# Fourier mixing before a mixture of experts: transforms without twiddle factors, and their 64x64 products in quarters of TensorE

## The chip, the cores and the metric

One core of a Trainium2 chip. Inputs and outputs lie in the chip's memory (HBM). The metric is the device time of one execution in microseconds. The kernel before takes 1613.09 us (median of 3 runs, 1611.04 to 1615.54).

## What is computed

```
batch, seq, dim = 8, 2496, 256;  N, D, E, F = 19968, 256, 8, 1024
X = np.fft.rfft(x, axis=1)                       # along the sequence
y = np.fft.irfft(X * (filt_r + 1j * filt_i), n=2496, axis=1)
x = y.reshape(N, D)
logits = x @ w_gate;  expert_idx = argmax(logits);  gate_w = softmax(logits)[expert_idx]
h = np.maximum(x_e @ w1[e], 0.0)                 # the rows of each expert e
out = gate_w[:, None] * (h @ w2[e])              # in the order of the tokens
```

All data is fp32. The kernel has two halves: a filter over the sequence, by a transform, a product and the transform back, for each of eight batches; and one expert of eight for each of the 19968 rows.

## The kernel before

*Filter.* 2496 is 39 x 64. A transform over 2496 points is made of 64 transforms over 39 points (stage A) and then, for each f of 0 to 19, one over 64 points (stage B); the remaining 19 values of f follow by symmetry, since x is real. Real and imaginary parts are rows of their own. The 256 columns of the data are the moving operand throughout, and the tables of cosines and sines are the weights.

- `stage_a` (L338): the three positions of the 64 that fill 117 rows at a time are multiplied by `tas` (117 x 120), 512 columns at a time (L344). The result `zo` goes to HBM (`zd`), because the next stage needs another distribution over partitions.
- `stage_b` (L351): for two values of f, two products of 256 columns with the 128 x 128 table of that f (L359). The twiddle factors, which a split into 39 and 64 needs, are in this table, so that there is one per f (`tbs`, 20 tables). Then VectorE multiplies by the filter: the product with its real part (L366), two products of half the partitions with its imaginary part, crosswise (L367, L368), and the sum (L370; in batch 0 on GpSimd).
- `stage_c` (L373): the 64-point transform back, with one table for all f but 0 (L384; L382 for f = 0 and 1), stored as `ud`.
- `stage_d` (L393): the 39-point transform back with a table for each of 22 groups (`tds`, which holds twiddle factors too), two products of 256 columns into a bank (L405), copied out as `yo`.
- `turn_y`, `logits`, `turn_logits`, `route` (L471 to L622): the result is turned and multiplied by `w_gate` (L491, four products of 32 output columns, in four strips of TensorE's columns), the expert and the row's place are found, and GpSimd scatters the rows to HBM, sorted by expert (L607).

Batch 0 goes another way, without HBM between the stages: `first_a` (L424), `turn_z` (L441), `stage_b`, `first_c` (L449), `turn_u` (L464) with the data kept in SBUF as `zt` and `ut`, turned by TensorE.

*Experts.* Tiles of 512, 256 and at the end 128 rows of one expert: `rows_in` loads them, `turn_x` (L737) turns them, `hidden` (L744) and `result` (L758) multiply with `w1` and `w2`, L748 and L763 evacuate, and GpSimd scatters to the output (L764).

*Order.* The order of TensorE, VectorE, ScalarE and the queue of SP is written out by the program (L913); GpSimd's is set by a scheduler. `slot(k)` lists the steps of the filter in which batch k is in stages B and C, batch k + 1 in A and batch k - 1 in D and the routing; each step has a place between 0 and 1 and a cost in us. A clock `now` advances by these costs. Between steps of the filter, expert steps are taken in: each filter step earns `share()` (L907, between 0.3 and 4) times its cost as credit. `stage_c` for one pair of f stands behind `stage_b` for the next. `either` (L234) gives each evacuation to VectorE or ScalarE, whichever would be free first by the program's reckoning; `stage_b` adds its vector work to that reckoning (L371). PSUM banks come from a pool of seven (L188), loads of x, z and u from a pool of seven buffers (`NIN`, L302).

Of the kernel before, what the change touches and what calls it, by code (L numbers as in the profile page):

```python
# [19 lines left out]
P = 128  # L20
S = 2496
# [3 lines left out]

N1 = 39
N2 = 64
NF = (N1 + 1) // 2
NS = 2 * NF

NB = 3
NG = 22
# [3 lines left out]
FT = F // P  # L36


def dft_tables():

    w = 2.0 * np.pi
    q = np.arange(N1)
    t = np.arange(N2)
    g = np.arange(N2)  # L50
    half = N2 // 2
    sg = np.where(g < half, 1.0, -1.0)

    ta = np.zeros((NB, N1, NB, NS))
    for f in range(NF):
        ang = w * ((q * f) % N1) / N1
        for j in range(NB):
            ta[j, :, j, f] = np.cos(ang)
            if f:
                ta[j, :, j, NF + f] = -np.sin(ang)  # L60

    tb = np.zeros((2, N2, NF, 2, N2))
    for f in range(NF):
        ang = w * ((t[:, None] * (f + N1 * g)[None, :]) % S) / S
        c, sn = np.cos(ang), np.sin(ang)
        if f:
            tb[0, :, f, 0] = c
            tb[1, :, f, 0] = sn
            tb[0, :, f, 1] = -sn * sg
            tb[1, :, f, 1] = c * sg  # L70
        else:
            tb[0, :, f, 0, :half] = c[:, :half]
            tb[0, :, f, 1, 1:half] = -sn[:, 1:half]
            tb[0, :, f, 0, half] = (-1.0) ** t

    tc = np.zeros((2, N2, 2, 2, N2))
    ang = w * ((g[:, None] * t[None, :]) % N2) / N2
    c, sn = np.cos(ang), np.sin(ang)
    tc[0, :, 1, 0] = c
    tc[0, :, 1, 1] = sn  # L80
    tc[1, :, 1, 0] = -sn * sg[:, None]
    tc[1, :, 1, 1] = c * sg[:, None]
    tc[0, :half, 0, 0] = 2.0 * c[:half]
    tc[1, :half, 0, 0] = -2.0 * sn[:half]
    tc[1, 0, 0, 0] = 0.0
    tc[0, 0, 0, 0] = 1.0
    tc[0, half, 0, 0] = (-1.0) ** t

    td = np.zeros((NB, NS, NG, NB, N1))
    ids = np.zeros((NB, N1, NG))  # L90
    valid = np.zeros((NB, N1, NG))
    for j in range(NB):
        for i in range(len(range(j, N2, NB))):
            n = N2 * q + NB * i + j
            ids[j, :, i] = n
            valid[j, :, i] = 1.0
            td[j, 0, i, j] = 1.0 / S
            for f in range(1, NF):
                ang = w * ((n * f) % S) / S
                td[j, f, i, j] = 2.0 / S * np.cos(ang)  # L100
                td[j, NF + f, i, j] = -2.0 / S * np.sin(ang)

    return {
        "ta": ta.reshape(TP, TK),
        "tb": tb.reshape(P, NF, P),
        "tc": tc.reshape(P, 2, P),
        "td": td.reshape(TK, NG, TP),
        "ids": ids.reshape(TP, NG),
        "valid": valid.reshape(TP, NG),
    }  # L110


def lay_x(x):

    out = np.zeros((x.shape[0], P, NG, D), x.dtype)
    v = x.reshape(-1, N1, N2, D)
    for j in range(NB):
        n = len(range(j, N2, NB))
        out[:, j * N1:(j + 1) * N1, :n] = v[:, :, j::NB]
    return out  # L120


def lay_filter(fr, fi):

    g = np.arange(N2)[:, None]
    f = np.arange(NF)[None, :]
    k = f + N1 * g
    k = np.where(k <= S // 2, k, S - k)
    fr, fi = fr[k], fi[k]
    h = NF // 2  # L130
    return np.concatenate([np.concatenate([fr, fr]), np.concatenate([fi[:, :h], fi[:, h:]])], axis=1)
# [3 lines left out]
def kernel(  # L135
# [3 lines left out]
    filt: bass.AP,  # L139
# [5 lines left out]
    tcm: bass.AP,  # L145
    td: bass.AP,
    ids: bass.AP,
# [48 lines left out]
    tbs = cst.tile([P, NF, P], F32, name="tbs")  # L196
    tcs = cst.tile([P, 2, P], F32, name="tcs")
    tds = cst.tile([TK, NG, TP], F32, name="tds")

    ht = cst.tile([P, NF + NF // 2, D], F32, name="ht")  # L200
# [14 lines left out]
    pro = first.enter_context(tc.tile_pool(name="pro", bufs=2, side="right"))  # L215
    pools = {}
# [33 lines left out]
    FH = [(f0, 4) for f0 in range(0, NF, 4)]  # L250


    def load_filters(c):
        f0, n = FH[c]
        nc.sync.dma_start(out=tbs[:, f0:f0 + n], in_=tb[:, f0:f0 + n])
        nc.sync.dma_start(out=ht[:HP, f0:f0 + n], in_=filt[:HP, f0:f0 + n, :])
        half, f1 = divmod(f0, NF // 2)
        rows = slice(half * HP, (half + 1) * HP)
        nh = min(n, NF // 2 - f1)
        nc.sync.dma_start(out=ht[rows, NF + f1:NF + f1 + nh], in_=filt[rows, NF + f1:NF + f1 + nh, :])  # L260
        if nh < n:
            nc.sync.dma_start(out=ht[HP:, NF:NF + n - nh], in_=filt[HP:, NF:NF + n - nh, :])
        if c == 0:
            nc.sync.dma_start(out=tcs, in_=tcm)

    def load_rest():
        nc.sync.dma_start(out=tds, in_=td)
        nc.vector.memset(wg, 0.0)
        nc.sync.dma_start(out=wg[:, :, :E], in_=moe_w_gate.rearrange("(i p) e -> p i e", p=P))
        nc.sync.dma_start(out=ids0, in_=ids)  # L270
        nc.sync.dma_start(out=vld, in_=valid)
# [21 lines left out]
    def columns(ap, i0, n):  # L293

        rows = ap.rearrange("t s d -> (t s) d")
        m = min(n, NG - 1 - i0)
        yield TK, slice(0, m), rows[i0 * TK:(i0 + m) * TK, :].rearrange("(i p) d -> p i d", p=TK)
        if m < n:
            yield NS, slice(m, n), rows[(NG - 1) * TK:, :].rearrange("(i p) d -> p i d", p=NS)
# [26 lines left out]
    def load_z(b, c):  # L326
        f0, n = FH[c]
        zi = fin(("z", b, c))
        nc.sync.dma_start(out=zi[:HP, :n], in_=zd[b][:, f0:f0 + n, :])
        nc.sync.dma_start(out=zi[HP:, :n], in_=zd[b][:, NF + f0:NF + f0 + n, :])  # L330

    def load_u(b, c):
        i0, n = CH[c]
        ui = fin(("u", b, c))
        for r, m, v in columns(ud[b], i0, n):
            nc.sync.dma_start(out=ui[:r, m], in_=v)

    def stage_a(b, c):  # L338
        i0, n = CH[c]
        xt = ins.pop(("x", b, c))  # L340
        zo = sb.tile([TK, 4, D], F32, tag="st", name="zo", bufs=4)
        for j in range(0, n, 2):
            p = bank()
            mm(p[:TK, :], lhsT=tas, rhs=xt[:TP, j:j + 2, :], start=True, stop=True)  # L344
            evac(zo[:, j:j + 2, :], p[:TK, :].rearrange("p (t d) -> p t d", t=2), 512)
        for r, m, v in columns(zd[b], i0, n):
            move(v, zo[:r, m])
# [3 lines left out]
    def stage_b(b, f):  # L351
        c, j = divmod(f, 4)
        if b == 0:
            zi, j = outs.pop(("zi", f)), 0
        else:
            zi = ins["z", b, c] if j == 0 else ins.pop(("z", b, c))
        p = bank()
        for i in range(2):
            mm(p[:, i * D:(i + 1) * D], lhsT=tbs[:, f + i, :], rhs=zi[:, j + i, :], start=True, stop=True)  # L359

        z2 = p.rearrange("p (i d) -> p i d", i=2)
        ys = outs["y", b, f] = sb.tile([P, 2, D], F32, tag="ys", name="ys", bufs=3)
# [618 lines left out]
```

## Time and profile before

| | |
|---|---|
| median of 3 runs | 1613.09 us |
| profiled execution, its own time | 1628.11 us |
| span in the profile | 1626.4 us |
| mean granted TensorE clock | 0.987 |
| TensorE busy | 1570.7 us, 7094 instructions |
| weight loads busy | 1143.6 us |
| VectorE, ScalarE, GpSimd busy | 423.1, 518.5, 358.2 us |
| expert products L744, L758 | 592.0 + 503.9 + 83.2 us busy |
| filter products L344, L359, L384, L405 | 74.5, 73.2, 67.0, 77.6 us busy |
| moved by DMA | 289.89 MB, mean 178 GB/s |

A group in the profile is a line, an engine, an operation and the tiles: `bank<-ys,tcs` is a product with moving operand ys and table tcs into a PSUM bank. "Busy" counts overlapping instructions once; a "mean ns of one" contains the instruction's latency, so that a pipelined instruction appears longer than its share of the time. Text in brackets or after the second bar says how long the engine was idle before, and whose end released it. A fp32 product appears as two matmul instructions, a transposition as one. In the timeline, slot 0 begins at 18.7 us (the first L441), slot 1 about 56 us, slot 2 about 125 us, slot 3 about 195 us, slot 4 about 300 us; the first expert tile is turned at 164.5 us, and after some 1050 us only experts are left.

### The profile page before, as it was taken

To read this page: it belongs to the slowest core of one execution; us is meant where nothing else is said; L and a number is where in the kernel's file an instruction comes from. 1 tells how busy PE (TensorE), PEld (TensorE's weight loads), DVE (VectorE), ACT (ScalarE), POOL (GpSimd) and SP (SyncE) were. 2 spreads that over 40 slices of the span, in tenths; PEclk is the share of its full clock that TensorE was granted. 3 is DMA by queue.
4 is the path that set the end of the run, shared out by engine and by line. 5 is a ranking of instruction groups with operands and counts; after the bars stand their busy time and mean duration, and the time that the engine had idled before them with its cause. 6 is when DMAs were issued, how large, how long until landed. Compare 5 with 4: busy or idle time off the path is not lost.

```text
span 1626.4 us, 21714 instructions
## 1 busy us (share of the span) xinstructions
PE 1570.7 (97%) x7094; PEld 1143.6 (70%) x7094; DVE 423.1 (26%) x1418; ACT 518.5 (32%) x1149; POOL 358.2 (22%) x373
## 2 busy tenths in 40 slices
PE   8988899999999999999999899999999999999998
PEld 6645667787566666666666566667666678889997
DVE  4676571624412422235222111300000000000000
ACT  4434343333322232322233232122222222333433
POOL 1131312404213321023213205411111011111111
PEclk9999999999999999999999999999999999999999
DMA  9679796887935584357434624433344347565551
GB/s 283 185 198 293 234 329 196 244 262 241 289 121 163 167 250 138 114 152 191 144 106 129 178 89 142 145 112 112 133 151 153 129 142 229 187 214 184 172 182 46
DMA packets 119700, 289.89 MB, mean 178 GB/s; under 512 B 17387, under 2 KB 58484, under 8 KB 119469
## 3 DMA queue, kind: packets, MB, share of 16 engines
q1 hardware_dynamic: 100373, 245.18, 49.9%
q0 software_dynamic: 19216, 43.33, 7.7%
q8 instruction: 58, 0.95, 0.2%
q14 instruction: 53, 0.43, 0.1%
HBM read 208.44 MB, written 80.90 MB: 178 GB/s over the span
## 4 chain that ended last, share of the span: by engine, by line
PE 90%; DMA 4%; DVE 3%; issue 2%; SPq 0%; ACT 0%; POOL 0%; POOLq 0%; ACTq 0%; DVEq 0%
PE bank L758 34%; PE bank L744 34%; PE bank L405 4%; PE bank L359 3%; PE bank L344 3%; PE bank L384 3%; PE bank L737 2%; PE bank L477 2%; DMA fin<-zd 1%; PE lt L491 1%; DMA fin<-ud 1%; DMA ud<-uo 1%; PE bank L424 1%; DVE yw L368 1%; DVE yw L367 1%
## 5 line engine op out<-in xcount | busy, mean ns | idle before, releaser
L744 PE MATMUL bank<-xT,w1t 128*128 128x512 f32 (+2 forms) x2080 | 592.0, 436 | 0.0
L758 PE MATMUL bank<-w2t,hT 128*128 128x256 f32 x2240 | 503.9, 382 | 2.6 <-issue 2.6
L744 PEld LDWEIGHTS bank<-xT,w1t 128*128 128x128 f32 x2080 | 338.9, 191 | 206.2 <-issue 183.7
L758 PEld LDWEIGHTS bank<-w2t,hT 128*128 128x128 f32 x2240 | 423.9, 191 | 70.2 <-issue 14.2
L764 POOL DMA_INDIRECT out_dram<-ys,idt x163 | 160.6, 985 | 917.2 <-ACT ys L763 624.4
L748 ACT ACTIVATE hT<-bank 128x512 f32<-128x512 f32 (+2 forms) x520 | 227.3, 438 | 369.3 <-PE bank L744 333.4
L607 POOL DMA_INDIRECT rows<-yo,row x176 | 175.5, 997 | 303.5 <-DVE row L587 73.6
L763 ACT ACTIVATE ys<-bank,gts 128x256 f32<-128x256 f32 x157 | 74.3, 474 | 500.0 <-PE bank L758 447.9
L241 DVE COPY xT<-bank 128x128 f32<-128x128 f32 (+2 forms) x53 | 25.1, 473 | 586.1 <-PE bank L737 459.6
L366 DVE TENSOR_TENSOR ys<-bank,ht 128x512 f32<-128x512 f32 x80 | 55.1, 689 | 131.0 <-PE bank L359 88.2
L405 PE MATMUL bank<-fin,tds 120*117 120x256 f32 (+1 forms) x308 | 77.6, 391 | 12.0 <-DMA fin<-ud 12.0
L758 PE MATMUL bank<-w2s,hT 128*128 x368 | 83.2, 379 | 0.0
L405 PEld LDWEIGHTS bank<-fin,tds 120*117 120x117 f32 (+1 forms) x308 | 55.6, 185 | 37.0 <-issue 20.4
L384 PE MATMUL bank<-ys,tcs 128*128 128x512 f32 x126 | 67.0, 614 | 10.8 <-DVE ys L370 6.1
L344 PE MATMUL bank<-fin,tas 117*120 117x512 f32 x154 | 74.5, 603 | 0.0
L758 PEld LDWEIGHTS bank<-w2s,hT 128*128 128x128 f32 x368 | 68.1, 190 | 8.3
L359 PE MATMUL bank<-fin,tbs 128*128 128x256 f32 x280 | 73.2, 385 | 0.8 <-DMA fin<-zd 0.8
L359 PEld LDWEIGHTS bank<-fin,tbs 128*128 128x128 f32 x280 | 52.3, 192 | 21.5 <-issue 15.5
L241 ACT COPY uo<-bank 128x512 f32<-128x512 f32 x70 | 41.1, 587 | 62.7 <-PE bank L384 36.7
L367 DVE SCALAR_TENSOR_TENSOR yw<-bank,ht 64x512 f32<-64x512 f32 x80 | 55.4, 693 | 1.1
L368 DVE TENSOR_TENSOR yw<-bank,ht 64x512 f32<-64x512 f32 x80 | 54.7, 684 | 1.1
L241 ACT COPY yo<-bank 117x512 f32<-117x512 f32 x70 | 40.6, 589 | 40.7 <-PE bank L405 38.5
(126 smaller groups left out, 877.6 us busy)
## 6 DMA issues: line engine op xcount, KB each, us to landing
w1t<-in_moe_w_dram SPq DMA_DIRECT2D x130, 512.0 KB
w2t<-in_moe_w_dram SPq DMA_DIRECT2D x84, 512.0 KB
fin<-in_x_dram SPq DMA_DIRECT2D x40, 512.0 KB
fin<-zd SPq DMA_DIRECT2D x70, 256.0 KB
ud<-uo SPq DMA_DIRECT2D x70, 256.0 KB
zd<-zo SPq DMA_DIRECT2D x35, 480.0 KB
fin<-ud SPq DMA_DIRECT2D x35, 480.0 KB
xg<-rows SPq DMA_DIRECT2D x28, 544.0 KB
```

Source lines behind the costliest of these rows:

```text
L241: either(n, lambda: nc.vector.tensor_copy(o, i), lambda: nc.scalar.copy(out=o, in_=i))
L344: mm(p[:TK, :], lhsT=tas, rhs=xt[:TP, j:j + 2, :], start=True, stop=True)
L359: mm(p[:, i * D:(i + 1) * D], lhsT=tbs[:, f + i, :], rhs=zi[:, j + i, :], start=True, stop=True)
L367: nc.vector.scalar_tensor_tensor(out=yw[:HP], in0=z2[HP:], scalar=-1.0, in1=fi, op0=ALU.mult, op1=ALU.mult)
L384: mm(p, lhsT=tcs[:, 1, :], rhs=ys, start=True, stop=True)
L405: mm(p[:TP, i * D:(i + 1) * D], lhsT=tds[:k, i0 + j + i, :], rhs=ui[:k, j + i, :], start=True, stop=True)
L607: sc = nc.gpsimd.indirect_dma_start(out=rowsd, out_offset=bass.IndirectOffsetOnAxis(ap=at, axis=0), in_=what, in_offset=None,)
L744: mm(p[:, :m], lhsT=w1t[2 * i + k // FH2][:, dh, k % FH2 * P:(k % FH2 + 1) * P], rhs=xts[i][:, dh, :m], start=(dh == 0), stop=(dh == DH - 1))
L748: lambda: nc.scalar.activation(hT[:, :m], p[:, :m], AF.Relu))
L758: mm(p[:, :D], lhsT=hs[i][k][:, j * P:(j + 1) * P], rhs=w2, start=(k == 0), stop=(k == FT - 1))
L763: lambda: nc.scalar.activation(ys, p[:, :D], AF.Copy, scale=gate))
L764: nc.gpsimd.indirect_dma_start(out=out, out_offset=bass.IndirectOffsetOnAxis(ap=idt[i].bitcast(U32)[:, j, :], axis=0), in_=ys, in_offset=None,
```

## The change

Since 39 and 64 have no common factor, the 2496 positions can be indexed by their remainders, and then the two-dimensional transform needs no twiddle factors. One table serves all f in stage B, one all groups in stage D.

- Positions t and t + 32 of the 64 are added and subtracted first (`add_x`, on GpSimd; the difference of batch 0 on VectorE); the sums give the even, the differences the odd half of the 64-point transform, each over 32 points. Real and imaginary parts of 32 points are 64 rows, so a table is 64 x 64.
- `stage_a` keeps its 512 moving columns a product; its two products of a chunk are the sums and the differences.
- `stage_b` now handles four values of f (q = 0 to 4) at a time: four products of 64 x 64 with 512 columns, in the four quarters of TensorE: o (even or odd half) chooses the rows and the PSUM bank, e (which two of the four f) the output partitions. The filter: a multiplication by the real part for each bank on VectorE (128 x 512), eight copies of 32 x 512 on ScalarE that exchange real and imaginary part, one multiplication by the imaginary part with its sign (128 x 1024) on VectorE, the sum (128 x 1024) on GpSimd.
- `stage_c` is four quarter products likewise, and two evacuations. In batch 0, `first_c` uses a table of 128 x 128 with zeros (`tc0`).
- `stage_d` multiplies one 512-column operand of both halves with the one table; ScalarE copies the even half out, VectorE adds and subtracts the odd half.
- The filter comes in two tables, `hr` and `hi` (128 x 20 x 256 each); GpSimd multiplies `hi` by signs as it is loaded. The copies of the filter on ScalarE in batch 0 (L435) are gone.
- z is loaded and u stored in four DMAs for each q (before: two for each four f). `share()` may reach 12. Small tiles of `tile_map` are shared, and `ys` of the experts has three buffers for four.

```
     def load_filters(q):
...
+        nc.sync.dma_start(out=hr[:, q], in_=filt_r[:, q])
+        nc.sync.dma_start(out=hi[:, q], in_=filt_i[:, q])
+        nc.gpsimd.tensor_tensor(hi[:, q], hi[:, q], sgs[:, q, :, None].to_broadcast((P, 4, D)), op=ALU.mult)
...
+    def quarter(ap, q, h):
+        return ap.rearrange("(h t) (q e c j) d -> h q c t e (j d)", h=2, q=NQ, e=2, c=2)[h, q]
...
+    def load_z(b, q):
+        zi = fin(("z", b, q))
+        for h in range(2):
+            rows = zi[h * HP:(h + 1) * HP]
+            for c in range(2):
+                nc.sync.dma_start(
+                    out=rows[c * HB:(c + 1) * HB].rearrange("t (e j) d -> t e (j d)", e=2), in_=quarter(zd[b], q, h)[c])
...
+    def add_x(b, c):
+        m = CH[c][1] // 2
+        xt = ins["x", b, c]
+        xs = xss[b, c] = sb.tile([TP, 2, D], F32, tag="xs", name="xs", bufs=2)
+        lo, hi_ = xt[:TP, :m], xt[:TP, m:2 * m]
+        nc.gpsimd.tensor_tensor(xs[:, :m], lo, hi_, op=ALU.add)
+        (nc.vector if b == 0 else nc.gpsimd).tensor_tensor(hi_, lo, hi_, op=ALU.subtract)
+        free["p"] = max(free["p"], now[0]) + (1.3 if b == 0 else 2.6)
...
     def stage_a(b, c):
...
-        for j in range(0, n, 2):
-            p = bank()
-            mm(p[:TK, :], lhsT=tas, rhs=xt[:TP, j:j + 2, :], start=True, stop=True)
+        for h, v in enumerate((xs[:, :m, :], xt[:TP, m:2 * m, :])):
+            p = bank()[:TK, :m * D]
+            mm(p, lhsT=tas, rhs=v, start=True, stop=True)
...
+    def stage_b(b, q):
+        zi = outs.pop(("zi", q)) if b == 0 else ins.pop(("z", b, q))
+        po = [bank(), bank()]
+        for e in range(2):
+            for o in range(2):
+                rows = slice(o * HP, (o + 1) * HP)
+                mm(po[o][e * HP:(e + 1) * HP, :], lhsT=tbs[rows, :], rhs=zi[rows, 2 * e:2 * e + 2, :], start=True, stop=True)
+        ys = outs["y", b, q] = sb.tile([P, 2, 2 * D], F32, tag="ys", name="ys", bufs=2)
+        yw = sb.tile([P, 2, 2 * D], F32, tag="yw", name="yw", bufs=2)
+        for o in range(2):
+            nc.vector.tensor_mul(ys[:, o], po[o], hr[:, q, 2 * o:2 * o + 2].rearrange("p j d -> p (j d)"))
+            for r in range(0, P, HB):
+                nc.scalar.copy(out=yw[r:r + HB, o], in_=po[o][r ^ HB:(r ^ HB) + HB])
+        nc.vector.tensor_mul(yw, yw, hi[:, q].rearrange("p (o j) d -> p o (j d)", o=2))
+        nc.gpsimd.tensor_tensor(ys, ys, yw, op=ALU.add)
+        free["s"] = max(free["s"], now[0]) + 4.7
+        free["v"] = max(free["v"], now[0]) + 2.6
+        free["p"] = max(free["p"], now[0]) + 2.5
...
+    def stage_c(b, q):
+        ys = outs.pop(("y", b, q))
+        uo = sb.tile([P, 4, D], F32, tag="st", name="uo", bufs=4)
+        pe = [bank(), bank()]
+        for o in range(2):
+            for e in range(2):
+                rows = slice(e * HP, (e + 1) * HP)
+                mm(pe[e][o * HP:(o + 1) * HP, :], lhsT=tcs[rows, o, :], rhs=ys[rows, o, :], start=True, stop=True)
+        for e in range(2):
+            evac(uo[:, 2 * e:2 * e + 2, :], pe[e].rearrange("p (j d) -> p j d", j=2), 512)
+        for h in range(2):
+            for c in range(2):
+                r = h * HP + c * HB
+                move(quarter(ud[b], q, h)[c], uo[r:r + HB].rearrange("t (e j) d -> t e (j d)", e=2))
...
     def stage_d(b, c):
...
+        for i in range(m):
             p = bank()
+            mm(p[:TP, :], lhsT=tds[:k, :], rhs=uv[:, i], start=True, stop=True)
+            even = sb.tile([TP, D], F32, tag="even", name="even", bufs=2)
+            nc.scalar.copy(out=even, in_=p[:TP, :D])
+            nc.vector.tensor_tensor(yo[:, i, :D], p[:TP, D:], even, op=ALU.add)
+            nc.vector.tensor_tensor(yo[:, m + i, :D], even, p[:TP, D:], op=ALU.subtract)
...
     def slot(k):
...
+            for q in range(NQ + 1):
+                at = q / (NQ + 1)
+                if q < NQ:
+                    steps.append((at, lambda q=q: stage_b(k, q), ("z", k, q), 0.95))
+                if q >= 1:
+                    steps.append((at + 0.01, lambda q=q: stage_c(k, q - 1), None, 0.95))
         if k + 1 < B:
             for c in range(nch):
+                at = (0.25 if k == 0 else 0.0) + 0.7 * c / nch
+                steps.append((at - 0.1, lambda c=c: add_x(k + 1, c), ("x", k + 1, c), 0.0))
+                steps.append((at, lambda c=c: stage_a(k + 1, c), ("x", k + 1, c), 0.43 * CH[c][1]))
...
-        return min(4.0, max(0.3, (known - RESERVE) / max(left_t[0], 1.0)))
+        return min(12.0, max(0.3, (known - RESERVE) / max(left_t[0], 1.0)))
```

## The prediction

> **What bounds the kernel now.** I read the page's busy shares and chain first, then the groups by shape, then the PE timeline. TensorE is the bound, and two thirds of its chain are expert products (L744, L758), which the change leaves alone.
>
> ```profile
> PE 1570.7 (97%) x7094; PEld 1143.6 (70%) x7094; DVE 423.1 (26%) x1418; ACT 518.5 (32%) x1149; POOL 358.2 (22%) x373
> ...
> PE 90%; DMA 4%; DVE 3%; issue 2%; SPq 0%; ACT 0%; POOL 0%; POOLq 0%; ACTq 0%; DVEq 0%
> ```
>
> PE idles 1626.4 - 1570.7 = 55.7 us. Busy time by stretch puts 22 of these before 140 us, 13 more before 240 us and 5.8 after 1500 us: filters are added in little time that others could hide at the start, and in much later. The groups that change, and the durations I use (in the groups, the column after the bar is busy us, mean ns):
>
> ```profile
> L384 PE MATMUL bank<-ys,tcs 128*128 128x512 f32 x126 | 67.0, 614 | 10.8 <-DVE ys L370 6.1 <-DVE pos L582 2.9 <-issue 1.7
> L359 PE MATMUL bank<-fin,tbs 128*128 128x256 f32 x280 | 73.2, 385 | 0.8 <-DMA fin<-zd 0.8
> ...
> L491 PE MATMUL lt<-yt,wg 128*32 128x234 f32 x352 | 25.3, 376 | 0.0
> ...
> L366 DVE TENSOR_TENSOR ys<-bank,ht 128x512 f32<-128x512 f32 x80 | 55.1, 689 | 131.0 <-PE bank L359 88.2 <-issue 13.3 <-PE bank L744 9.4
> L370 DVE TENSOR_TENSOR ys<-ys,yw 128x512 f32<-128x512 f32 x70 | 48.5, 694 | 2.4
> L370 POOL TENSOR_TENSOR ys<-ys,yw 128x512 f32<-128x512 f32 x10 | 12.7, 1268 | 40.0 <-DVE yw L368 26.8 <-PE bank L344 7.9 <-PE bank L359 5.2
> ```
>
> Each fp32 product is two PE instructions (77 products of L344 are 154 records). Mean durations contain pipeline latency, so I take start to next start from the timeline (start us, us to the end of the last):
>
> ```profile
> 71.84 1.89 PE L405 MATMUL bank<-ui,tds 120*117 120x256 f32 x8
> 73.66 1.01 PE L491 MATMUL lt<-yt,wg 128*32 128x234 f32 x16
> 74.60 1.02 PE L477 MATMUL bank<-ident,yo 117*128 117x117 f32 x8
> 75.46 1.04 PE L359 MATMUL bank<-fin,tbs 128*128 128x256 f32 x4
> 76.33 0.38 PE L464 MATMUL bank<-ident,ut 128*120 128x128 f32 x2
> ...
> 111.77 1.10 PE L384 MATMUL bank<-ys,tcs 128*128 128x512 f32 x2 [2.85 <-DVE pos L582]
> 112.70 1.03 PE L359 MATMUL bank<-fin,tbs 128*128 128x256 f32 x4
> 115.16 1.12 PE L384 MATMUL bank<-ys,tcs 128*128 128x512 f32 x2 [1.43 <-DVE ys L370]
> 117.98 2.04 PE L384 MATMUL bank<-ys,tcs 128*128 128x512 f32 x2 [1.70 <-issue]
> 119.82 1.91 PE L359 MATMUL bank<-fin,tbs 128*128 128x256 f32 x4
> ```
>
> L359 takes 75.46 to 76.33 = 0.87 us for two columns, L384 0.86. L491 puts eight products of 32 output columns into 0.94 us, though its 16 passes in a row would take 16 x 0.197 = 3.1 us (0.43 us per 512 moving columns): four strips run at once. The last lines show PE waiting for the filter multiplication, and then running at half speed.
>
> **What the skill says.** "TensorEngine Tiling (Array Packing)", Tiling Modes: tiles run independently, and a change of tiling mode drains TensorE. L491 agrees on both: four passes per strip are 0.79 us, so a visit costs 0.15 us more, and 0.10 before it (its predecessor's 8 x 0.215 us end at 73.56). No run here shows row tiles. "TensorE: Matmul & The Clock Gate", Part 1: idling halves the clock for a while; the 2.04 us above agree. Same part: ScalarE, VectorE and GpSimd queues are strict FIFO; nothing in the trace contradicts it. "GPSIMD Engine Reference", 3.1, price: 4497 ns for a two-input add of 2048 elements. With L370's 1268 for 512 that is 2.10 ns an element: an estimate of 2.34 us for 1024, 0.73 for 256.
>
> **The change, part by part.**
>
> *Quarter products.* A group (four columns f) costs B 1.74, C 1.72 us now. After: four quarters, two passes of 512 each, 0.86 us if all four overlap, plus 0.15 to 0.25: I take 1.07. Bounds: 0.95, and 2 x 0.86 + 0.25 = 1.97 if row tiles take turns. Saving: 35 groups x (0.67 + 0.65) + batch 0's five B x 0.67 = 46.2 + 3.3 = 49.5 us.
>
> *Stages A and D.* As many moving columns as before: 0. D's evacuation (0.59 us per 512) becomes a copy of 256 (0.38) and two vector operations (0.43 each); the turn of the result comes some 0.7 us later, behind at least one more D chunk of 1.72 us: 0, or 0.7 x 12 where that cover is gone. Turns and batch 0's other products keep their counts.
>
> *The chain from B to C, in batches 1 to 7.* Now: four vector operations, 0.69 each, with handovers 3.0 us. After: first multiplication 0.69, eight copies of 32 x 512 on ScalarE (in the built order each set of four waits for VectorE; two copies back to back take 1.05, so 0.46 apart: 7 x 0.46 + 0.59 = 3.81), a multiplication of 1024 (0.69 + 512/0.96 ns = 1.23), the add on GpSimd 2.34, handovers 0.6: 8.7 us. The PE work standing between B and its C in the built order, against that length (a wait already taken lengthens the next column's cover):
>
> - batch 1: covers 17.4, 6.2, 5.6, 3.0, 1.1 us, waits 2.5 + 0.6 + 5.1 + 2.5 = 10.7
> - batch 2: 4.5, 8.3, 11.8, 8.6, 3.2: 9.7. Batch 3: 8.4, 18.7, 11.8, 8.6, 3.2: 5.8
> - batches 4 to 7: shortest covers 6.6, 6.3, 8.1, 1.1: 2.1 + 2.4 + 0.6 + 7.6 = 12.7
>
> Sum 38.9. The same table of the old order at 3.0 us gives 9.2 (6.2 in batch 1, where the trace has 1.28 + 0.18 + 2.85 + 1.43 + 1.70 = 7.4). So 29.7 more. What stands behind the waiting C on PE is everything: stage A, D, experts.
>
> *Batch 0.* GpSimd gets the first add of x (1.27, on the path to the first product), the sign multiplications of the filter (2.34 each), both x operations of batch 1 (2.54 a chunk), the filter adds (2.34). The first filter add can start at 21.5 (end of B now) + 1.3 + 8.7 - 2.4 = 29.1. Behind it in the queue stand 4 x 2.34 + 4 x 2.54 + 1.46 + 4 x 2.34 = 30.4: the last ends at 29.1 + 2.3 + 30.4 = 61.8, now 53.70 + 1.26 = 55.0. So 7 us later, and the 3.3 saved there is not seen: 10.3.
>
> *Given back.* In slots 2 and 3 PE now idles 2.35 + 0.47 + 0.29 + 0.37 + 4.54 + 3.99 = 12 us for transfers and routing; these go on while PE waits at C: -12 (bounds 0, -12).
>
> *Clock.* The waits before 118 us made the next three rows 1.02 + 0.88 + 1.28 = 3.2 us longer. Two more such clusters: 6.4 (bounds 0, 12).
>
> *DMA.* Tables shrink, filters grow, sum within 0.3 MB. Each z load and u store has two more DMAs, half as long: 140 issues of some 0.4 us on SP, ahead of x, u and weight loads; seven buffers of lead hide them: 0. *Share limit 4 to 12, smaller tiles:* they move expert work, which is in the covers already: 0.
>
> Sum: -49.5 + 29.7 + 10.3 - 12 + 6.4 = -15.1 us. The profiled execution (span 1626.4, time 1628.1) would become 1613.0; it lies 15.0 above the median of the runs shown, 1613.1, which becomes **1598.0**.
>
> **Rivals.**
> 1. *Expert work covers the waits* (1574): ScalarE and GpSimd turn out faster, or C falls later. Then only batch 0 loses: 1613.1 - 49.5 + 10.3. For it: covers of 12 to 80 us in the middle of batches 4 to 7. Against: the short ones at their ends.
> 2. *All is given back* (1613): no overlap with transfers (+12) and a third clock cluster (+3.2).
> 3. *Slower, by GpSimd's queue* (1630): the filter adds stand behind scatters in the built order, mostly blocks of six to eight at 1.0 us (L607), each block waiting for routing. If 16 of the 40 C wait 2 us longer, that is +32. It decides from (15.1 + 4.8)/16 = 1.25 us each. For it: the page has POOL waiting for DVE row 73.6 us in nine waits. Against: most scatters start while the chain is still on ScalarE.
> 4. *The quarters don't all overlap* (1666): row tiles take turns, 1.97 us a group: +0.23 x 40 + 0.25 x 35 = +18 in place of -49.5. Against: L491.
>
> **How the numbers follow.** Faster or slower starts at 0.3% (4.8 us), about what a measurement of this kernel can tell from no change. Forecast 0.42 (own range 1586 to 1609), rival 1 0.25, rival 2 0.12, rival 3 0.16, rival 4 0.05. Faster 0.40 + 0.25 = 0.65, same 0.02 + 0.12 = 0.14, slower 0.21. The range leaves out rival 4, half of rival 3 and a quarter of rival 1: 1564 to 1632.
>
> **What would show it.** Right: groups of four quarters about 1.07 us from start to next start; eight copies in about 3.8 us; PE waits of 3 to 8 us ahead of the C products, released by POOL, some 39 us in sum; batch 0's last filter add near 62 us; after 1050 us nothing changed. Wrong: groups near 2 us (rival 4); waits at C under 10 us in sum (rival 1) or over 60 (rival 3).

## The result and the profile after

The changed kernel takes **1762.61 us** (median of 4 runs, 1760.76 to 1764.16), the kernel before 1612.53 (4 runs, 1611.04 to 1615.54): the ratio is 1.093, with a 95% interval of 1.091 to 1.095. The prediction said 1598.0 with a range up to 1632, so it is wrong in sign, and no rival reached so far. The profiled execution of the changed kernel has a span of 1762.4 us, 136.0 more than that of the kernel before; the medians differ by 150.1, since the profiled execution of the kernel before was itself 15.6 us above its median, so that comparisons of the two traces are good to some 15 us.

Of the page of the changed kernel: the busy line, the granted clock in 40 slices of 44 us each, and the chain that ended last.

```profile
PE 1577.6 (90%) x7058; PEld 1059.7 (60%) x7058; DVE 458.3 (26%) x1490; ACT 635.0 (36%) x1382; POOL 556.2 (32%) x498
...
PEclk9787668789997989999998999999999999999999
...
PE 72%; ACT 3%; DVE 3%; DMA 2%; issue 2%; POOL 2%; SPq 0%; POOLq 0%; DVEq 0%; ACTq 0%
```

TensorE idles 1762.4 - 1577.6 = 184.8 us, where it idled 55.7: **+129.1 us**. Its busy time is 6.9 us longer, although its quarters are at least as short as predicted (shown below), that is 49.5 us less work. The remainder, 49.5 + 6.9 = **56.4 us**, I put down to a slower clock. The stretches of the trace give about the same size in another way: the sum, over seven stretches, of busy time by one minus the clock is 73.9 us after and 15.7 before, 58.2 more (50 to 58 with equal stretches of 11 to 88 us). TensorE's share of the chain fell from 90% to 72%.

The stretch from 130 to 400 us holds most of it. Columns: length, busy time of PE, PEld, DVE, ACT and POOL with instructions, then the clock, the DMA share and GB/s. The kernel before:

```profile
130.00:400.00 270.00, 253.24 (x1193) 184.82 (x1193) 130.33 (x445) 101.60 (x225) 75.41 (x76) 0.97 0.83 256
```

The changed kernel:

```profile
130.00:400.00 270.00, 172.34 (x717) 83.14 (x712) 124.73 (x370) 112.92 (x228) 129.31 (x104) 0.77 0.70 213
```

There are 80.9 us less of busy TensorE, and what is left runs at 0.77. No other engine is full (GpSimd, whose busy time grew most, is at 48%). So no engine became the bound by its sum of work; operations wait for each other in line. The first expert tile is turned at 364.89 us, where it was 164.5, so there is no expert work to put between the steps of the filter. After 1100 us TensorE is full in both.

What TensorE waited for in the changed kernel (us in total, times, longest us):

```profile
PE bank L389 <- POOL xs L378: 38.7, 7, 13.3
PE bank L424 <- POOL ys L412: 30.3, 6, 8.5
PE bank L389 <- DVE av_i L673: 15.9, 2, 7.9
...
PE lt L533 <- ACT yt L266: 12.0, 5, 5.4
PE bank L389 <- DMA ud<-uo: 11.2, 2, 11.0
PE bank L403 <- DVE zi L266: 10.8, 4, 3.3
PE bank L472 <- POOL seg L303: 9.6, 1, 9.6
```

Only the second row is the wait for the filter at C, which the prediction had put at 38.9 us for batches 1 to 7; it is 30.3. The largest place is stage A (L389), which never waited before: 67.7 us in front of the sums of x and 3.2 in front of the differences. D (L445) waits hardly at all. By groups of the changed kernel:

```profile
L445 PE MATMUL bank<-fin,tds 120*117 120x512 f32 (+1 forms) x154 | 78.8, 631 | 0.1
L389 PE MATMUL bank<-xs,tas 117*120 117x512 f32 (+1 forms) x84 | 48.9, 668 | 67.7 <-POOL xs L378 38.7 <-DVE av_i L673 15.9 <-DMA ud<-uo 11.0
L389 PE MATMUL bank<-fin,tas 117*120 117x512 f32 (+1 forms) x84 | 48.2, 661 | 3.2 <-POOL fin L379 2.0 <-POOL hi L283 0.9 <-DMA ud<-uo 0.2
```

The names `av_i` and `ud` mislead here: they are what happened to end last. Each of these three long waits (8.0, 7.9 and 11.0 us) ends within 0.1 us of GpSimd's sum of x. One of them, in the changed kernel:

```profile
230.45 0.72 POOL L378 TENSOR_TENSOR xs<-fin 117x256 f32<-117x256 f32 x1
...
231.23 1.21 PE L389 MATMUL bank<-xs,tas 117*120 117x256 f32 x2 [7.95 <-DVE av_i L673]
```

The same engines at work in batch 0, from the timeline of the changed kernel (start, us to the end):

```profile
43.60 1.58 PE L403 MATMUL bank<-zi,tbs 64*64 64x512 f32 x8 [1.63 <-DVE zi L266]
...
46.63 1.22 DVE L408 TENSOR_TENSOR ys<-bank,hr 128x512 f32<-128x512 f32 x2
47.36 4.71 ACT L410 COPY yw<-bank 32x512 f32<-32x512 f32 x8 [5.22 <-DVE ys L408]
...
52.15 1.23 DVE L411 TENSOR_TENSOR yw<-yw,hi 128x1024 f32<-128x1024 f32 x1 [4.29 <-issue]
53.29 1.28 DVE L266 COPY zi<-bank 128x512 f32<-128x512 f32 x2
53.45 2.35 POOL L412 TENSOR_TENSOR ys<-ys,yw 128x1024 f32<-128x1024 f32 x1 [1.17 <-DVE yw L411]
54.12 1.12 PE L403 MATMUL bank<-zi,tbs 64*64 64x512 f32 x2 [3.24 <-DVE zi L266]
```

This is the trap. VectorE issues its multiplication by the real part, and next in its queue stands the multiplication by the imaginary part (L411), which must wait for eight copies on ScalarE (4.71 us, to 52.07). VectorE is idle for 4.29 us. Behind L411 stands the copy of `zi`, the input of the *next* B. So B follows B in 54.12 - 43.60 = 10.5 us, TensorE stands 3.24 us before it, and batch 0's last filter add ends at 77.2 us, not at 61.8. In the whole kernel VectorE waited so 36 times, and GpSimd's sum waited for VectorE in turn (the changed kernel's waits of these engines):

```profile
DVE yw L411 <- ACT yw L410: 150.3, 36, 4.2
...
POOL ys L412 <- DVE yw L411: 126.8, 25, 11.6
```

Later, GpSimd's queue shows the same thing one step on. TensorE and then GpSimd about 300 us, changed kernel:

```profile
297.98 1.04 PE L424 MATMUL bank<-ys,tcs 64*64 64x512 f32 x8
312.31 2.06 PE L389 MATMUL bank<-xs,tas 117*120 117x512 f32 x2 [13.29 <-POOL xs L378]
```

```profile
299.87 1.01 POOL L649 DMA_INDIRECT rows<-yo,row  x1 [6.85 <-DVE cnt L630]
301.19 0.99 POOL L649 DMA_INDIRECT rows<-yo,row  x1 [0.30 <-issue]
...
309.98 0.98 POOL L649 DMA_INDIRECT rows<-yo,row  x1 [0.30 <-issue]
310.98 1.27 POOL L378 TENSOR_TENSOR xs<-fin 117x512 f32<-117x512 f32 x1
```

GpSimd waited 6.85 us for routing on VectorE (`cnt`), then issued eight scatters, most of them 1.3 us apart, and only then added x for stage A. TensorE stood for 13.29 us.

One more thing is in the page's DMA issues, which neither the diff's words nor the prediction had. `todo`, the list of loads, takes the key of every step; since `add_x` and `stage_a` have the same key, each x is loaded **twice**: 80 loads of 512 KB instead of 40 (and 16 of 256 KB instead of 8), and 313.27 MB moved instead of 289.89. The changed kernel, then the kernel before:

```profile
fin<-in_x_dram SPq DMA_DIRECT2D x80, 512.0 KB, 6.0
```

```profile
fin<-in_x_dram SPq DMA_DIRECT2D x40, 512.0 KB
```

### The profile page after: what moved, and what is told of

Same layout as the page of the kernel before. It is cut to its first block, busy times and chain, and to the rows that moved or that the text cites. A ratio compares the mean times of both kernels' runs of the same rounds, so it can differ in the third digit from the quotient of the medians.

```text
span 1762.4 us, 22497 instructions
## 1 busy us (share of the span) xinstructions
PE 1577.6 (90%) x7058; PEld 1059.7 (60%) x7058; DVE 458.3 (26%) x1490; ACT 635.0 (36%) x1382; POOL 556.2 (32%) x498
## 2 busy tenths in 40 slices
DMA packets 139238, 313.27 MB, mean 178 GB/s; under 512 B 21871, under 2 KB 62992, under 8 KB 139121
## 4 chain that ended last, share of the span: by engine, by line
PE 72%; ACT 3%; DVE 3%; DMA 2%; issue 2%; POOL 2%; SPq 0%; POOLq 0%; DVEq 0%; ACTq 0%
PE bank L801 31%; PE bank L787 30%; ACT yw L410 3%; PE bank L445 2%; PE bank L780 2%; PE bank L389 2%; PE bank L519 1%; PE lt L533 1%; PE bank L403 1%; POOL rows L649 1%; DMA fin<-in_x_dram 1%; PE bank L424 1%; DMA w2t<-in_moe_w_dram 1%; DVE ys L408 0%; POOL xs L378 0%
## 5 line engine op out<-in xcount | busy, mean ns | idle before, releaser
L787 PE MATMUL bank<-xT,w1t 128*128 128x512 f32 (+2 forms) x2080 | 597.2, 441 | 17.0 <-issue 13.3
L410 ACT COPY yw<-bank 32x512 f32<-32x512 f32 x320 | 184.3, 576 | 100.5 <-DVE ys L408 96.7
L412 POOL TENSOR_TENSOR ys<-ys,yw 128x1024 f32<-128x1024 f32 x40 | 94.0, 2349 | 171.1 <-DVE yw L411 126.8
L389 PE MATMUL bank<-xs,tas 117*120 117x512 f32 (+1 forms) x84 | 48.9, 668 | 67.7 <-POOL xs L378 38.7
L411 DVE TENSOR_TENSOR yw<-yw,hi 128x1024 f32<-128x1024 f32 x40 | 51.5, 1287 | 167.3 <-ACT yw L410 150.3
L445 PE MATMUL bank<-fin,tds 120*117 120x512 f32 (+1 forms) x154 | 78.8, 631 | 0.1
L378 POOL TENSOR_TENSOR xs<-fin 117x512 f32<-117x512 f32 (+1 forms) x48 | 56.6, 1180 | 58.2 <-PE bank L389 31.1
L408 DVE TENSOR_TENSOR ys<-bank,hr 128x512 f32<-128x512 f32 x80 | 51.4, 684 | 80.3 <-PE bank L403 78.7
L424 PE MATMUL bank<-ys,tcs 64*64 64x512 f32 x280 | 42.5, 680 | 30.3 <-POOL ys L412 30.3
L389 PEld LDWEIGHTS bank<-xs,tas 117*120 117x120 f32 x84 | 14.9, 208 | 85.8 <-POOL xs L378 71.6
L449 DVE TENSOR_TENSOR yo<-bank,even 117x256 f32<-117x256 f32 x88 | 37.1, 422 | 75.7 <-ACT even L448 73.2
L519 PEld LDWEIGHTS bank<-ident,yo 117*128 117x128 f32 x352 | 41.1, 150 | 25.1 <-issue 16.2
```

The costliest lines, as they stand in the source:

```text
L389: mm(p, lhsT=tas, rhs=v, start=True, stop=True)
L410: nc.scalar.copy(out=yw[r:r + HB, o], in_=po[o][r ^ HB:(r ^ HB) + HB])
L412: nc.gpsimd.tensor_tensor(ys, ys, yw, op=ALU.add)
L424: mm(pe[e][o * HP:(o + 1) * HP, :], lhsT=tcs[rows, o, :], rhs=ys[rows, o, :], start=True, stop=True)
L445: mm(p[:TP, :], lhsT=tds[:k, :], rhs=uv[:, i], start=True, stop=True)
L519: nc.tensor.transpose(pt[:, 2 * i + dh, :TP], yo[:, j + i, dh * P:(dh + 1) * P], ident[:TP, :TP])
```

## The experiments

The theory after this profile: the chain between B and C with its eight copies is the main cost, by its length or by what stands behind it in VectorE's queue. The rivals: GpSimd's queue (sums of x, filter sums, scatters), and the doubled loads of x. Where an expectation says theory A, it means the exchange by copies, and theory B is GpSimd's queue. All ratios are to the kernel before, run beside the version in question on the same chip; its medians lie between 1608.43 and 1627.08 us. "Points" are hundredths of this ratio. A difference in points between versions measured on different chips takes it that a chip slows both kernels alike, which was not tested.

### The rivals first, one at a time, on the changed kernel

*x loaded once:*

```
-    todo = [step[2] for step in STEPS if step[2] and step[2] != "y"]
+    todo = list(dict.fromkeys(step[2] for step in STEPS if step[2] and step[2] != "y"))
```

> Each chunk of x is loaded once (the changed kernel's list of loads names it twice, so 96 loads of x stand on the queue where 48 did before). If the doubled loads are the main loss (22.5 MB more, and two of seven load buffers for one chunk): at most 1700 us, from 1763. If the queues of the engines are (GpSimd, VectorE behind ScalarE's copies): 1740 to 1760, since only the start and some z and u loads come earlier.

Measured: 1739.91 us, ratio 1.081 (1.076 to 1.087), 1.2 points less: the loads are not the main loss. PE's wait for the sums of x falls from 38.7 to 3.5 us, but waits for the filter sum (39), for `oe` and `zi` on VectorE and for `yt` on ScalarE (15 to 18 each) grow.

*Sum and difference of x on VectorE:*

```
-        nc.gpsimd.tensor_tensor(xs[:, :m], lo, hi_, op=ALU.add)
-        (nc.vector if b == 0 else nc.gpsimd).tensor_tensor(hi_, lo, hi_, op=ALU.subtract)
+        nc.vector.tensor_tensor(xs[:, :m], lo, hi_, op=ALU.add)
+        nc.vector.tensor_tensor(hi_, lo, hi_, op=ALU.subtract)
```

> Sum and difference of x on VectorE in every batch, all else as in the changed kernel. If GpSimd's queue is the main loss: PE's waits for the sums and differences of x (39 + 2 us) go, with the slow clock after them some 60 us, so about 1700. If the doubled loads are: no more than 10 us. If VectorE's queue behind ScalarE's copies is: no gain or slower, since the two operations then stand in that queue.

Measured: 1760.67 us, 1.094 (1.091 to 1.097): nothing. The waits are now for `xs` on VectorE, 61.6 us.

*Filter sum on VectorE:*

```
-        nc.gpsimd.tensor_tensor(ys, ys, yw, op=ALU.add)
+        nc.vector.tensor_tensor(ys, ys, yw, op=ALU.add)
```

> The sum of the filter on VectorE in place of GpSimd, all else as in the changed kernel. If the chain from B to C over GpSimd is the main loss: PE's waits for this sum (30 + 4 us) go and the chain is 1.1 us shorter and free of the scatters: about 1715. If the sums and differences of x on GpSimd are: 1740 to 1760.

Measured: 1764.31 us, 1.096 (1.093 to 1.100): no gain, which neither case of the expectation foresaw; waits for the sum move from POOL to DVE (23.9 us), those for the sums of x grow to 45.6.

*x loaded once, and its sums on VectorE:*

> Loads of x once and sum and difference of x on VectorE. If the two losses are separate, the gains of the two single edits add up; if they hide each other (a late x waits for whichever is later), the gain is more than their sum. By the theory of GpSimd's queue about 1690, by that of the doubled loads about 1690 too, by neither above 1740.

Measured: 1757.7 us, 1.092 (1.088 to 1.096), so the two together give less than the first alone. What is taken off GpSimd now waits on VectorE: PE stands 50.9 us for `xs` there. Taken out one at a time, with the copies still in place, no rival gives back more than 1.2 points of 9.3.

### The copies

*Two copies of 128 x 512 for eight of 32 x 512*, so that real and imaginary part are not exchanged:

```
-            for r in range(0, P, HB):
-                nc.scalar.copy(out=yw[r:r + HB, o], in_=po[o][r ^ HB:(r ^ HB) + HB])
+            nc.scalar.copy(out=yw[:, o], in_=po[o])
```

> Two copies of 128 x 512 in place of eight of 32 x 512; it leaves out the exchange of real and imaginary parts, so the filter is not applied as it should be. ScalarE's copies take 1.2 us a group in place of 4.7. Theory A (VectorE and ScalarE hand over to each other in strict order: the multiplication by the imaginary part stands directly behind the one by the real part in VectorE's queue and holds up everything behind it, 150 us in all): the wait falls to some 0.5 us, most of the loss returns, 1640 to 1670. Theory B (GpSimd's queue): the sums only come 3.5 us earlier, 1720 to 1750.

Measured: 1701.9 us, 1.046 (1.042 to 1.051), between the two ranges expected. Half of the loss goes with six copies. (Rows may now go to other experts, but TensorE has the same 7058 instructions.) VectorE's wait for them falls from 150.3 to 23.8 us; PE now waits for the sums of x most, 77.0 us where it was 38.7. So the largest row of waits grows while the time falls: a row is not a cause.

*All copies kept, but L411 and the sum issued half a period later, as a step of their own*, so that other work of VectorE goes ahead:

```
+    def stage_b2(b, q):
+        ys, yw = outs["y", b, q], outs.pop(("w", b, q))
+        nc.vector.tensor_mul(yw, yw, hi[:, q].rearrange("p (o j) d -> p o (j d)", o=2))
+        nc.gpsimd.tensor_tensor(ys, ys, yw, op=ALU.add)
```

> All eight copies stay; the multiplication by the imaginary part and the sum are issued as a step of their own, about half a period of the filter later, so that other evacuations stand between on VectorE. Theory A: VectorE's waits for the copies (150 us) fall below 40, and 50 us or more return: at most 1710. If ScalarE's load alone (184 us of copies) is the loss: no change within 15 us, since the copies stay. Theory B: no gain, the sum comes later.

Measured: 1763.01 us, 1.084 (1.080 to 1.088). This missed: I had expected the place in VectorE's queue to be most of it. VectorE's wait for the copies falls from 150.3 to 13.3 us, but the sum comes later, and PE waits for it 57.2 us. The time in us is that of the changed kernel; by the ratio it is 0.9 points less. The expectation's other case, that ScalarE's load alone is the loss, foresaw no change too; but TensorE waits only 16 us for ScalarE in this trace (25 in the changed kernel), far less than for the sum. At the one place tried, the better place in the queue was paid for by a longer chain.

*The kernel before with such copies:* its two crosswise multiplications (L367, L368) are replaced by four copies of 32 x 512 and one multiplication, by the real table instead of the imaginary; transforms and tables stay.

```
-        nc.vector.scalar_tensor_tensor(out=yw[:HP], in0=z2[HP:], scalar=-1.0, in1=fi, op0=ALU.mult, op1=ALU.mult)
-        nc.vector.tensor_mul(yw[HP:], z2[:HP], fi)
+        for r in range(0, P, 32):
+            nc.scalar.copy(out=yw[r:r + 32], in_=z2[(r + HP) % P:(r + HP) % P + 32])
+        nc.vector.tensor_mul(yw, yw, ht[:, f:f + 2, :])
```

> The kernel before, with its two crosswise multiplications replaced by four copies of 32 x 512 on ScalarE and one multiplication on VectorE that waits for them (it multiplies by the real part's table where the imaginary part's belongs). Its transforms, products and loads stay. Theory A: the same exchange of hands alone makes it slower by 60 us or more (80 pairs of columns, 2.4 us of waiting each, about half of it in PE's way). If the loss comes from the new transforms, the doubled loads or GpSimd: within 15 us of before, since VectorE has 0.7 us a pair less to do.

Measured: 1698.58 us, 1.044 (1.039 to 1.049). The old transforms, with no additions of x and with x loaded once, lose 4.4% by this exchange alone (TensorE has the same 7094 instructions); VectorE's wait for ScalarE, in this kernel:

```profile
DVE yw L369 <- ACT yw L368: 178.3, 72, 2.9
```

### The exchange made by TensorE

*The changed kernel with nothing changed but the exchange* (and B's cost in the written-out order, now 1.8 us): a second set of four quarters in B, with the columns of the table exchanged, gives real and imaginary part crosswise in two more banks, and VectorE multiplies straight from there. It costs 40 groups by 0.9 us, 36 us of TensorE.

```
+        px = [bank(), bank()]
+        for s, out_ in enumerate((po, px)):
             for e in range(2):
                 for o in range(2):
                     rows = slice(o * HP, (o + 1) * HP)
-                    mm(po[o][e * HP:(e + 1) * HP, :], lhsT=tbs[rows, :], ...)
+                    mm(out_[o][e * HP:(e + 1) * HP, :], lhsT=tbs[rows, s * N2:(s + 1) * N2], ...)
...
+            nc.vector.tensor_mul(yw[:, o], px[o], hi[:, q, 2 * o:2 * o + 2].rearrange("p j d -> p (j d)"))
```

> The changed kernel in everything (x loaded twice, sums and differences of x and filter sum on GpSimd), but the exchange of real and imaginary parts made by a second set of quarter products in B instead of copies on ScalarE. If the copies are the main loss, 1.035 to 1.05: what the same version with x loaded once takes (1.0281), and 1.2 to 1.6 points for the second load. If the copies are one loss among several that only hurt together, 1.06 or more.

Measured: 1696.76 us, **1.045** (1.044 to 1.047). From 1.093, the exchange by copies costs 4.8 points more than the exchange by TensorE with its 36 us (about 2.2 points, if those are on the path). This is the copies as a whole: their length, what waits behind them on VectorE, and their room in ScalarE's queue.

*The same with x loaded once:*

> The version with the exchange made by more quarter products in B (1.0088), with the filter sum on GpSimd in all batches as in the changed kernel. If the copies on ScalarE and what queues behind them are the whole loss, it stays within 0.3 points, 1.006 to 1.012. If GpSimd's sum in the chain (2.34 us, behind scatters) has a share, 1.015 to 1.03, with PE waiting for POOL ys 20 us or more.

Measured: 1658.56 us, 1.028 (1.026 to 1.030): 1.7 points for the second load.

*The same, and the filter sum on VectorE in batches 1 to 7:*

> The exchange is made by TensorE: four more quarter products with the table's columns exchanged give the parts the other way round, and VectorE multiplies straight from PSUM; no copies. x loaded once; the sum on VectorE from batch 1 on. PE gets 0.9 us a group more, 35 us in all. Theory A: without any handover between VectorE and ScalarE the loss goes: 1600 to 1650. Theory B: x operations and scatters still share GpSimd, so 1690 or more.

Measured: 1642.44 us, 1.009 (1.007 to 1.011): 1.9 points for GpSimd's sum, which gave nothing on the changed kernel. (As timed, the two versions are only 16 us apart; the kernel before took 1627.08 us beside this one and 1613.28 beside the other.) The version before waited 22.2 us for POOL at C; here that row is gone.

*The doubled loads on the kernel before* (each key of x twice in `todo`):

> The kernel before, with each block of x loaded twice into two buffers, as the changed kernel does (23 MB more to read). If the doubled loads cost time by themselves, the ratio to the kernel before is about 1.012, what loading once gained on the changed kernel. If they only hurt where filters already run late, 1.000 to 1.005.

Measured: 1638.97 us, 1.016 (1.014 to 1.018). They cost time by themselves, even with the short chain of the old transforms (DMA is busy 0.99 of the first 60 us there, where it was 0.86); the expectation's other case is out.

*No exchange and no sum in batches 1 to 7,* x loaded once: both products of the filter go to C, which adds them in PSUM with a second table, whose rows are exchanged. Batch 0 keeps the second set of quarters in B; some small tiles are moved or shared to make room.

```
+        for s, v in enumerate((ys, yw)):
             for o in range(2):
                 for e in range(2):
                     rows = slice(e * HP, (e + 1) * HP)
-                    mm(pe[e][o * HP:(o + 1) * HP, :], lhsT=tcs[rows, o, :], rhs=ys[rows, o, :], start=True, stop=True)
+                    mm(pe[e][o * HP:(o + 1) * HP, :], lhsT=tcs[rows, 2 * s + o, :], rhs=v[rows, o, :],
+                       start=s == 0, stop=s == 1)
```

> x loaded once; in batches 1 to 7 there is no exchange and no sum at all: VectorE multiplies the result of B by the real and by the imaginary part straight from PSUM (four operations of 128x512), and C adds both products in PSUM with a second table (four more quarters, 0.9 us a group). Batch 0 as in the version with a second set of quarters in B. If the length of the elementwise chain is what costs, it is 2.9 us here, about that of the kernel before, and the ratio is 0.995 to 1.009 (49.5 us saved, 36 us of quarters added, the rest of the start's losses). If what is left lies with GpSimd's additions of x and the later result of D, it stays at 1.009 or above, with PE waiting for POOL xs and DVE.

Measured: 1613.86 us, 1.001 (0.9997 to 1.002).

*With sums and differences of x on VectorE as well:*

> The version whose C adds two products, with sums and differences of x on VectorE too, whose queue is shorter by the filter sum. If GpSimd's queue still costs, 0.3 to 0.8 points below that version. If VectorE becomes the queue to wait in, as in the changed kernel with x on VectorE, 0 to 0.5 points above it, with waits for DVE xs.

Measured: 1610.93 us, **0.9992** (0.998 to 1.000). The gain of 0.2 points is smaller than the first case of the expectation and on the other side of the second. VectorE, which was the worse place for x in the changed kernel once x was loaded once (1.092 for 1.081), is now no worse. The page of this kernel:

```profile
PE 1556.7 (97%) x7378; PEld 1052.1 (65%) x7378; DVE 418.1 (26%) x1498; ACT 515.9 (32%) x1184; POOL 368.1 (23%) x373
```

With the prediction's saving, 1570.7 - 49.5 + 36 is 1557.2, beside 1556.7 measured: the saving is there in TensorE's busy time. That it fits to half a us is in part luck, since a group takes less than the 1.07 us of the prediction (below). But the way without copies spends 36 of the 49.5 us again, and of what is left only 2 us show in the time; where the rest goes was not found. This is as fast as the kernel before, and not shown to be faster.

### Are the copies free where expert work stands beside them?

*Batches 1 to 3 as in the last kernel, batches 4 to 7 with the eight copies and GpSimd's sum* (20 groups by 0.9 = 18 us less for TensorE). Rival 1 spoke of covers of 12 to 80 us in the middle of these batches.

> The version whose C adds two products, with x on VectorE (0.9992), in batches 1 to 3; in batches 4 to 7 B and C as in the changed kernel, with eight copies on ScalarE and the sum on GpSimd. The quarters saved are 20 groups by 0.9 = 18 us. If expert work covers the long chain there, 0.988 to 0.995 (faster than both kernels). If the chain's places with short cover take it back (four batches by 2 to 8 us, as the prediction's table had them, or more behind scatters), 1.000 or above, with waits of PE for POOL ys after 400 us.

Measured: 1666.25 us, 1.026 (1.024 to 1.027). They are not free. PE waits in this kernel:

```profile
PE bank L394 <- DVE xs L383: 24.7, 6, 9.2
PE rk L607 <- DVE oe L596: 14.7, 8, 3.3
PE bank L462 <- DMA fin<-ud: 12.5, 2, 8.7
PE bank L440 <- POOL ys L429: 6.8, 2, 6.2
```

At C (L440), where the prediction looked, there are only 6.8 us. More stands on VectorE: the sums of x for stage A (L383) and the expert's number for the ranks (`oe`), 24.7 and 14.7 us, where the kernel without copies waits 11.0 and 3.4.

*The same, with the waiting multiplication and the sum later in their queues:*

> The version with the copies in batches 4 to 7 only (1.0255), where the multiplication by the imaginary part and the sum are issued some third of a period after B as a step of their own, so that other work of VectorE stands between the copies and them. If the place in VectorE's queue is the loss there, waits for DVE xs, DVE oe and the loads behind them shrink from some 50 us to under 15, and with 18 us of quarters saved the ratio is 0.988 to 1.002. If the chain's length is the loss, PE waits for POOL ys at C instead (7 us so far, then 20 or more) and the ratio stays at 1.012 or above.

Measured: 1642.28 us, 1.016 (1.014 to 1.018), 0.9 points less than with the multiplication in its old place. The ratio and the wait at C are those of the expectation's second case, the shorter waits for VectorE those of its first. PE waits in this kernel:

```profile
PE bank L446 <- POOL ys L435: 26.4, 6, 8.5
PE bank L394 <- DVE xs L383: 7.7, 6, 3.1
...
PE rk L613 <- DVE oe L602: 1.8, 5, 0.6
```

The waits for VectorE shrink by 30 us, those at C grow by 20. So both halves of the theory exist, the place in the queue and the length of the chain; in the two orders tried, most of what one gives the other takes.

## Why the prediction was wrong

The step that failed is how the new chain was priced: by PE's waits at C alone, with nothing for what stands behind the waiting L411 on VectorE and nothing for stage A, whose operand had become the work of a waiting engine. These waits, batch 0's and the clock were 29.7 + 10.3 + 6.4 = 46.4 us in the sum; measured are 129.1 us more idle time and some 56 us of slower clock, and replacing the copies alone gives back 4.8 points.

- **Quarter products, -49.5 us: right.** I took 1.07 us a group and expected that all four quarters overlap. From the timeline of the changed kernel, B takes 324.90 - 324.00 = 0.90 us and C 0.97 from start to next start; a group alone between other products takes 1.02 (at 819.96 us). By these figures the saving is an estimated 53 to 60 us; rival 4 (the quarters take turns) is out. "TensorEngine Tiling (Array Packing)" of the Trainium skill, Tiling Modes, says that tiles run independently; for row tiles, which no run before showed, this trace agrees.

```profile
324.00 1.09 PE L403 MATMUL bank<-fin,tbs 64*64 64x512 f32 x8
324.90 1.04 PE L424 MATMUL bank<-ys,tcs 64*64 64x512 f32 x8
325.87 1.55 PE L445 MATMUL bank<-fin,tds 120*117 120x512 f32 x3
```

- **"Stages A and D: 0": D right, A wrong.** D (L445) waits 0.1 us. A waits 70.9 us, over half of the new idle time. I had counted A's moving columns, and not that its operands now come from GpSimd, behind scatters that wait for routing on VectorE. That this routing is late because of the copies is not shown. That A is where the time passes doesn't make it the cause: with x loaded once the waits for its sums fall to 3.5 us and the kernel gains only 1.2 points; with six copies fewer they rise to 77.0 and it gains 4.6.
- **The chain from B to C: its length nearly right, what it holds up wrong: the failed step.** Eight copies take 4.70 us, not 3.81 (they stand 0.59 apart; the 0.46 came from one pair of other copies). The multiplication of 1024 takes 1.23 us and GpSimd's sum 2.35, as priced. (The 0.96 elements a ns behind the 1.23 come out of the trace of the kernel before: VectorE's copies of 128 x 512 and 128 x 256 take 692 and 425 ns there.) The waits at C are 30.3 us where I had 38.9; as the order of work is another by then, this nearness is in part luck. But the sum holds only what waits for the *end* of the chain. The prediction named what stands behind the waiting C on PE, and never what stands behind the waiting L411 on VectorE, although that is a wait that the change adds; in batch 0 it is `zi`, and so the next B. The weight of the copies among the causes is shown by their replacement alone (4.8 points) and by batches 4 to 7, where C waits 6.8 us and the kernel still loses 42 us against the version without copies (2.6 points), with 18 us less to multiply.
- **Batch 0, +10.3: mis-sized.** I took GpSimd's 30.4 us as the bound and got 61.8 us for the last sum. It ended at 77.2, since B follows B there in 9 to 11 us, by the round of B, VectorE, ScalarE, VectorE and `zi`. That round trip bounds batch 0, not an engine's sum.
- **Given back, -12: two thirds happened, and were lost among new waits.** The 8.0 us for loads of `ud`, `zd` and `rows` in these slots are gone, and D's later waits for `ud` too (12.0 us in the whole kernel before). The 3.99 us for `oe` did not go: TensorE now waits 5.8 us for it.
- **Clock, +6.4: some 56 measured.** I priced two more clusters of waits; TensorE waited in nearly every slot up to 400 us, at 0.74 to 0.89 of its speed. "TensorE: Matmul & The Clock Gate", Part 1, says that idling halves the clock for a while; this trace agrees in kind (a product of A takes 2.06 us right after the wait of 13.29 us, 1.02 elsewhere), and here a stage with many gaps pays for most of its length.
- **DMA, 0: wrong.** The second loads of x cost 1.2 points here and 1.6 on the kernel before, some 19 to 26 us. They follow from one line of `todo` and the same key in two steps, both in the code. The stores of A and the loads of D also come in twice as many pieces, which the prediction left out; the last kernel, level with the one before, has these too.
- **Rivals.** Rival 3 (slower, by GpSimd's queue, +32) had the sign. Its mechanism exists: with the copies out, taking the sum from GpSimd gains 1.9 points; and in the changed kernel, of C's wait of 6.86 us before 147.26, some 5 us are GpSimd's queue (L411 ends at 139.92, the sum starts at 144.87, behind scatters and sums of x). But moving the sum to VectorE there gains nothing: in 25 of 40 cases the sum stood waiting for L411, 126.8 us in all. So this rival did not decide. Rivals 1 and 2 fall: in batches 4 to 7 expert work does hide most of the waits at C, as rival 1 said, and the loss comes in elsewhere.

The sum -49.5 + 129.1 (idle) + 56.4 (clock) = 136.0 us closes because 56.4 is its remainder; with 53 to 60 us saved by the quarters the remainder is 60 to 67, more than the clock of the stretches shows, so that a part of it may be something else. How the 129.1 split between the causes can't be read from one trace, as the single changes show: 1.2, 0 and 0 points for three of them with the copies there, for two of these (loads, filter sum) 1.7 and 1.9 once the copies are out, and for the third (x on VectorE) no more than 0.2, within the intervals. The 0.8 points from 1.009 to 1.001 belong together to the sum and to the place where the second product is made. What the new share limit of 12 and the shared small tiles contribute was not tried; with both in it, the last kernel is level with the one before, so together they cost no more there than what its quarters save, some 14 us of TensorE.

## What to carry to other kernels

For each instruction that the change makes wait, list what is queued behind it on *its own* engine, and price the start of the next round, not only the end of this one: a long handover between two engines (A, B, A) sets a period, whatever the shares of busy time. Work that saves TensorE time but adds a step on another engine between two of its products has to be priced with the clock as well, for the gaps slow what is left. And test suspects again after the main one is out: a fix that gained nothing behind a longer delay gained 1.9 points here later. The longest row of waits says where the time passes; only a change that takes the suspect out says why.

## What I had not expected of the hardware

Eight copies of 32 x 512 from PSUM on ScalarE take 4.70 us, 0.59 each, as much for each as one of 128 x 512 (0.585 to 0.591 in this trace): the partitions left out save nothing. Two groups of quarters in a row, the second adding to the first in PSUM, take 0.85 and 0.97 us, with a change to full-size products only after the second: by this pair the change costs an estimated 0.1 us, and the adding nothing. From the last kernel (0.9992):

```profile
419.00 1.04 PE L433 MATMUL bank<-ys,tcs 64*64 64x512 f32 x8
419.85 1.04 PE L433 MATMUL bank<-yw,tcs 64*64 64x512 f32 x8
420.82 1.98 PE L455 MATMUL bank<-fin,tds 120*117 120x512 f32 x4
```
